# One core: float64 weights converted in even steps, unit results written in four pieces

## The chip, the cores and the metric

The kernel runs on one core of one Trainium2 chip. The metric is the device time of one execution in microseconds (us), the median of three runs. Below, PE is TensorE, DVE is VectorE, ACT is ScalarE, POOL is GpSimd and SP is the SyncE queue from which most transfers are issued. TensorE has two clock levels, 1.2 and 2.4 GHz; in the profile's rows the granted clock is 0.50 at the lower and 1.00 at the higher, and values between are means over a stretch.

## What is computed

Three stages follow one another, over 4 x 576 = 2304 tokens of width 512. The two weight matrices of the last stage, `w_in` and `w_out`, come as float64.

```python
def reference(**kw):
    attn = _attn_ref(q, k, v)            # 4 batches, 8 heads, 576 x 64, window of 64 keys
    x = attn.transpose(0, 2, 1, 3).reshape(2304, 512)
    x = _moe_ref(x, ...)                 # 8 experts, each token to the one of highest logit:
                                         #   gate * (relu(x @ w1[e]) @ w2[e]), 512 -> 1024 -> 512
    h = x @ w_in                         # 512 -> 2048, w_in float64
    return (h - tanh(h)) @ w_out         # 2048 -> 512, w_out float64
```

## The kernel before

**Attention** (`attention`) runs over 36 groups of four 128x128 score blocks. Beside it tokens are routed: `route_task` finds expert and gate, scaled rows go to `xs` in DRAM, and a table of units is made.

**The expert stage** (`moe`) works through 5 units, each up to 504 tokens of one expert (the last one 288), in 8 steps of 128 of the 1024 hidden columns: 40 steps, `p` = 0 to 39, `f` = `p` mod 8. A step multiplies twice: `l1` (PE into `ps_h`, 12 matmuls) and, for the step before, `l2` (into `ps_y`, 12 matmuls). The fp32 numbers are multiplied as high and low half: ACT rounds to the high half (`w1h`, `w2h`, `hh`, `xh`) and DVE subtracts to get the low half (`w1l`, `w2l`, `hl`, `xl`). Weights of step `p+3` and `p+2` are loaded by `wload` from SP into a ring of five buffers `r`, and a load waits until DVE has split the weights that lay there. At `f` = 7 the next unit's tokens are transposed on PE and split (`xsplit`, tiles `x`, `xh`, `xl`, four blocks in two buffers), and the results go to `ys` (`yevac`). At `f` = 2 of the next unit `ywrite` writes all of `ys` to `yd` in one DMA of 1008 KB, and the token ids, four bytes each, to `idd`. The next unit's tokens come by `xgather_task` (`xg`), four indirect DMAs issued from POOL.

**The conversion** (`conv_task`, a generator, one 512 KB block of float64 at a time, 16 of `w_in` and 16 of `w_out`) is a task among those that `Sched.pump` moves on. `conv_load` loads `raw` from SP (two buffers), one block ahead. `conv_low` turns the low word into a number on ACT (`cvr`); `conv_top` makes the fp32 of the high word in four DVE instructions (`cva`, L743 to L746, the first of them takes the absolute value); `conv_sum` adds the two on POOL (`cvw`, or `woutW` for the last 8 blocks, which stay whole). A block's high half (`winH`, `woutH`) is then made on ACT and its low half (`winL`, `woutL`) on DVE or POOL in turn. `cva`, `cvr` and `cvw` have one buffer each. The first ten blocks are converted during attention, the other 22 from `p` = 8 on, one in each step, at every `f`.

**The last stage** (`second`) goes over 6 chunks of 384 tokens and 16 blocks of hidden columns: `m2l1` (PE into `ps_g`, three buffers), `act1` (five ACT and five DVE instructions, the fourth of DVE, L1123, releases `ps_g`), `act2` (high half on ACT, low half on POOL), `m2l2` (into `ps_q`). In the first 8 steps the 8 blocks that stayed whole are split too, with the low half on POOL (L768). Its tiles take the place in SBUF of the expert stage's.

The order on each engine is the order in which the code issues; each engine's queue runs in order and waits for semaphores.

Of the kernel before, what the change touches and what calls it, by code (L numbers as in the profile page):

```python
# [23 lines left out]
NF1 = F // 128  # L24
# [20 lines left out]
CONV0 = 8  # L45
# [6 lines left out]
class Sched:  # L52


    def __init__(self):
        self.tasks, self.first = [], False

    def add(self, g, last=False):
        self.tasks.append([g, 0, last])
        if not self.first:  # L60
            self.tasks.sort(key=lambda t: t[2])
# [16 lines left out]
class Kernel:  # L78
    def __init__(self, tc, ap):
# [3 lines left out]
        self.woutH, self.woutW, self.conv_on = [], None, False  # L83
# [288 lines left out]
    def attention(self):  # L372
# [9 lines left out]
        for g in range(-2, NG + 2):  # L382
            n = g + 3
            self.useZ = g < NG
            if 0 < n < NG:
# [8 lines left out]
                if n == 6:  # L394
                    self.sched.add(self.conv_task(), last=True)
# [25 lines left out]
            self.sched.pump()  # L421

# [273 lines left out]
    def conv_task(self):  # L696
        tiles = [(0, f) for f in range(NF2)] + [(1, f) for f in range(NF2)]
        ready = lambda w, f: (f < NWA or self.conv_on) if w == 0 else f < len(self.woutH) or self.woutW
        raw, late = self.conv_load(*tiles[0]), None
        yield 3  # L700
        for i, (w, f) in enumerate(tiles):
            while not ready(w, f):
                yield
            nxt = tiles[i + 1] if i + 1 < len(tiles) else None
            cur, raw = raw, self.conv_load(*nxt) if nxt else None
            eng = self.nc.vector if i % 2 else self.nc.gpsimd
            r = self.conv_low(cur)
            if i < NWA:
# [3 lines left out]
                if late:  # L712
                    self.split_lo(hl, late[2], eng)
                a = self.conv_top(cur)
            else:
                a = self.conv_top(cur)
                if late:
                    self.split(*late, eng)
                yield
            late = self.conv_sum(w, f, a, r)  # L720
            yield
        if late:
            self.split(*late, self.nc.gpsimd)
        self.conv_done = True

# [12 lines left out]
    def conv_top(self, raw):  # L738
# [4 lines left out]
        v.tensor_scalar(a, hi, 0x7FFFFFFF, None, op0=ALU.bitwise_and)  # L743
# [23 lines left out]
    def split_lo(self, hl, w, eng):  # L767
        eng.tensor_tensor(hl[1], w, hl[0].bitcast(F32), op=ALU.subtract)  # L768

    def split(self, which, f, w, eng):  # L770
        self.split_lo(self.split_hi(which, f, w), w, eng)
# [27 lines left out]
    def xgather_task(self, u, Ti, k, rows=NT, spread=False):  # L799
# [3 lines left out]
        u.ids = mo.tile([BR, n], I32, name="ids", bufs=self.nbuf(4))  # L803
# [105 lines left out]
    def ywrite(self, u, yd, idd):  # L909
        self.nc.sync.dma_start(yd[:, :, bass.ds(u.c, u.C)], u.ys[:, :, : u.C])  # L910
        self.put_ids(idd, u.c, u)

    def moe(self):
# [8 lines left out]
        for p in range(N):  # L922
            self.conv_on = p >= CONV0
            if p == NF1 + 2:
                self.sched.tasks.sort(key=lambda t: not t[2])
                self.sched.first = True
# [26 lines left out]
            if i == 0:  # L953
                self.sched.pump()
# [335 lines left out]
```

## Time and profile before

| what | value |
|---|---|
| three timed runs | 850.59, 850.95, 854.36 us; median 850.95 us |
| the profiled execution | 853.73 us, of which 851.9 us span |
| PE busy | 780.5 us, 92% of the span |
| DVE, ACT, POOL busy | 77%, 61%, 34% of the span |

The span runs from the first to the last recorded instruction. Attention ends at about 165 us, the expert stage at about 430 us; the last stage fills the rest. "Busy" says nothing yet on what waits: that is read stage by stage, from the idle time of PE and what ended it.

### The profile page before, as it was taken

To read this page: it belongs to the slowest core of one execution; us is meant where nothing else is said; L and a number is where in the kernel's file an instruction comes from. 1 tells how busy PE (TensorE), PEld (TensorE's weight loads), DVE (VectorE), ACT (ScalarE), POOL (GpSimd) and SP (SyncE) were. 2 spreads that over 40 slices of the span, in tenths; PEclk is the share of its full clock that TensorE was granted. 3 is DMA by queue.
4 is the path that set the end of the run, shared out by engine and by line. 5 is a ranking of instruction groups with operands and counts; after the bars stand their busy time and mean duration, and the time that the engine had idled before them with its cause. 6 is when DMAs were issued, how large, how long until landed. Compare 5 with 4: busy or idle time off the path is not lost.

```text
span 851.9 us, 12816 instructions
## 1 busy us (share of the span) xinstructions
PE 780.5 (92%) x4183; PEld 677.4 (80%) x4183; DVE 656.4 (77%) x1144; ACT 522.3 (61%) x1246; POOL 285.8 (34%) x291
## 2 busy tenths in 40 slices
PE   7898989878997797899979999999999999999995
PEld 6877777657886686687969999999999999999993
DVE  4679986556397797767559888888888888888883
ACT  5878777623343443334467777777777777777772
POOL 3344443200252253231054424423423333333322
PEclk9999999989999898999999999999999999999998
DMA  6777975513376386393940101001001000000001
GB/s 143 182 185 193 234 160 138 168 62 125 121 232 162 116 229 192 122 228 113 194 64 1 37 1 38 29 10 38 28 10 38 20 20 31 17 11 13 25 2 41
DMA packets 119070, 80.35 MB, mean 94 GB/s; under 512 B 70688, under 2 KB 107040, under 8 KB 118994
## 3 DMA queue, kind: packets, MB, share of 16 engines
q1 hardware_dynamic: 115730, 69.81, 31.8%
q0 software_dynamic: 3264, 9.63, 3.4%
q8 instruction: 35, 0.57, 0.3%
q14 instruction: 41, 0.34, 0.1%
HBM read 62.10 MB, written 14.16 MB: 90 GB/s over the span
## 4 chain that ended last, share of the span: by engine, by line
PE 66%; DVE 14%; DMA 9%; ACT 4%; issue 3%; POOL 2%; SPq 1%; DVEq 0%; POOLq 0%; ACTq 0%
PE ps_g L1102 23%; PE ps_q L1145 23%; PE ps_h L864 7%; PE ps_y L881 6%; DMA raw<-in_wout 4%; ACT P L316 2%; PE ps_o L349 2%; DMA r<-in_w 1%; DVE nm L314 1%; PE ps_s L310 1%; DVE cva L744 1%; DVE w2l L855 1%; DVE w1l L855 1%; DMA idd<-ids 1%; DVE PT L334 1%
## 5 line engine op out<-in xcount | busy, mean ns | idle before, releaser
L1133 POOL TENSOR_TENSOR gl<-gv,gh 128x384 fp32r<-128x384 f32 x96 | 100.0, 1042 | 185.8 <-ACT gh L1132 185.6
L1102 PE MATMUL ps_g<-yh,winH 128*128 128x384 f32 x384 | 129.9, 338 | 6.0 <-DVE gt L1123 6.0
L1102 PE MATMUL ps_g<-yh,winL 128*128 128x384 f32 x384 | 129.9, 338 | 0.0
L1102 PE MATMUL ps_g<-yl,winH 128*128 128x384 f32 x384 | 129.9, 338 | 0.0
L1124 DVE COPY_PREDICATED gv<-gm,gt 128x384 f32<-128x384 int32 x96 | 112.1, 1167 | 9.9
L1145 PE MATMUL ps_q<-woutH,gl 128*128 128x512 f32 x288 | 114.1, 396 | 1.0 <-POOL gl L1133 1.0
L1145 PE MATMUL ps_q<-woutH,gh 128*128 128x512 f32 x288 | 114.2, 397 | 0.1
L1145 PE MATMUL ps_q<-woutL,gh 128*128 128x512 f32 x288 | 113.9, 395 | 0.0
L1132 ACT ACTIVATE gh<-gv 128x384 fp32r<-128x384 f32 x96 | 50.4, 525 | 102.7 <-issue 85.1
L1120 DVE SCALAR_TENSOR_TENSOR gv<-gu,ps_g 128x384 f32<-128x384 f32 x96 | 53.1, 553 | 43.4 <-ACT gt L1117 42.6
L1102 PEld LDWEIGHTS ps_g<-yh,winH 128*128 128x128 f32 x384 | 72.6, 189 | 10.5 <-DVE gt L1123 6.6
L1122 DVE SCALAR_TENSOR_TENSOR gv<-gs,gv 128x384 f32<-128x384 f32 x96 | 74.3, 774 | 3.3
L1102 PEld LDWEIGHTS ps_g<-yl,winH 128*128 128x128 f32 x384 | 72.7, 189 | 4.0
L1102 PEld LDWEIGHTS ps_g<-yh,winL 128*128 128x128 f32 x384 | 72.7, 189 | 0.0
L316 ACT ACTIVATE P<-ps_s,nm 128x128 f32<-128x128 f32 x144 | 50.9, 365 | 28.3 <-DVE nm L314 27.2
L753 ACT ACTIVATE cvr<-raw 128x512 int32<-128x512 uint32 x32 | 21.6, 675 | 72.2 <-POOL cvw L759 33.0
L1145 PEld LDWEIGHTS ps_q<-woutL,gh 128*128 128x128 f32 x288 | 54.5, 189 | 12.9
L1145 PEld LDWEIGHTS ps_q<-woutH,gl 128*128 128x128 f32 x288 | 54.3, 188 | 10.4 <-POOL gl L1133 1.7
L1145 PEld LDWEIGHTS ps_q<-woutH,gh 128*128 128x128 f32 x288 | 54.4, 189 | 9.3 <-ACT gh L1132 0.5
L1115 ACT ACTIVATE gs<-gu,pa 128x384 f32<-128x384 f32 x96 | 59.3, 617 | 3.1
L1121 DVE SCALAR_TENSOR_TENSOR gv<-gs,gv 128x384 f32<-128x384 f32 x96 | 58.1, 605 | 3.3
L1116 ACT ACTIVATE gs<-gu,pa 128x384 f32<-128x384 f32 x96 | 57.8, 602 | 1.6 <-DVE gv L1122 1.6
(254 smaller groups left out, 1737.5 us busy)
## 6 DMA issues: line engine op xcount, KB each, us to landing
r<-in_w SPq DMA_DIRECT2D x80, 256.0 KB, 3.8
raw<-in_win SPq DMA_DIRECT2D x16, 512.0 KB, 5.3
raw<-in_wout SPq DMA_DIRECT2D x16, 512.0 KB, 3.6
xs<-r SPq DMA_DIRECT2D x18, 256.0 KB, 2.6
kr<-in_k SPq DMA_DIRECT2D x32, 128.0 KB, 2.7
qr<-in_q SPq DMA_DIRECT2D x32, 128.0 KB, 3.8
va<-in_v SPq DMA_DIRECT2D x32, 128.0 KB, 3.1
yd<-ys SPq DMA_DIRECT2D x4, 1008.0 KB, 14.1
```

The source lines that it names most:

```text
L316: nc.scalar.activation(P[:, j, :], ps[:, j, :], AF.Exp, bias=nm[:, j : j + 1], accum_out=sm[:, j : j + 1])
L864: nc.tensor.matmul(ps, w[:, c, :], x[:, c, :n], start=(c == 0 and i == 0), stop=(c == 3 and i == 2))
L881: nc.tensor.matmul(u.y[d], w[:, d * 128 : d * 128 + 128], x, start=(f == 0 and i == 0), stop=(f == NF1 - 1 and i == 2),)
L1102: nc.tensor.matmul(ps, w[:, c, :], x[:, c, :], start=(c == 0 and i == 0), stop=(c == 3 and i == 2))
L1115: nc.scalar.activation(s1, u, AF.Square, bias=self.pa1)
L1116: nc.scalar.activation(s2, u, AF.Square, bias=self.pa2)
L1120: nc.vector.scalar_tensor_tensor(v, u, cA, ps, op0=ALU.mult, op1=ALU.mult)
L1121: nc.vector.scalar_tensor_tensor(v, s1, b1, v, op0=ALU.add, op1=ALU.mult)
L1122: nc.vector.scalar_tensor_tensor(v, s2, b2, v, op0=ALU.add, op1=ALU.mult)
L1124: nc.vector.copy_predicated(v, m.bitcast(I32), t)
L1133: nc.gpsimd.tensor_tensor(gl, v, gh.bitcast(F32), op=ALU.subtract)
L1145: nc.tensor.matmul(self.po[t], g[:, sl], w, start=(f == 0 and i == 0), stop=(f == NF2 - 1 and i == 2))
```

## The change

`conv_task` leaves the scheduler's list. `conv_step` moves it on by hand: once in each attention group, so that a block still takes two groups, and in the expert stage twice per step, one block, only at `f` = 1 to 6 and from `p` = 4 on. Blocks are loaded two ahead: at the end of block `i` block `i+2` is loaded, into the buffer that block `i` has just left. From the tenth block on the absolute value is made on ACT instead of DVE. All low halves are made on DVE, those at the start of the last stage too. `ywrite` writes one of the four column blocks of `ys` at each of `f` = 1, 2, 3 and 4, and the ids with the fourth. The ids' tile moves from the expert stage's pool to the constants.

```diff
-CONV0 = 8
+CONV0 = 4
+CONVF = (1, 2, 3, 4, 5, 6)
...
-                    self.sched.add(self.conv_task(), last=True)
+                    self.conv = self.conv_task()
...
             self.sched.pump()
+            self.conv_step()
...
-        raw, late = self.conv_load(*tiles[0]), None
+        raws, late = [self.conv_load(*t) for t in tiles[:2]], None
         yield 3
         for i, (w, f) in enumerate(tiles):
             while not ready(w, f):
                 yield
-            nxt = tiles[i + 1] if i + 1 < len(tiles) else None
-            cur, raw = raw, self.conv_load(*nxt) if nxt else None
-            eng = self.nc.vector if i % 2 else self.nc.gpsimd
+            cur = raws.pop(0)
             r = self.conv_low(cur)
             if i < NWA:
                 if late:
                     hl = self.split_hi(*late)
                 yield
                 if late:
-                    self.split_lo(hl, late[2], eng)
-                a = self.conv_top(cur)
+                    self.split_lo(hl, late[2])
+                a = self.conv_top(cur, False)
             else:
-                a = self.conv_top(cur)
+                a = self.conv_top(cur, True)
                 if late:
-                    self.split(*late, eng)
+                    self.split(*late)
                 yield
             late = self.conv_sum(w, f, a, r)
+            if i + 2 < len(tiles):
+                raws.append(self.conv_load(*tiles[i + 2]))
             yield
...
-        v.tensor_scalar(a, hi, 0x7FFFFFFF, None, op0=ALU.bitwise_and)
+        hf = raw.bitcast(F32).rearrange("p (n two) -> p n two", two=2)[:, :, 1]
+        if act:
+            self.nc.scalar.activation(x, hf, AF.Abs)
+        else:
+            v.tensor_scalar(a, hi, 0x7FFFFFFF, None, op0=ALU.bitwise_and)
...
-    def split_lo(self, hl, w, eng):
-        eng.tensor_tensor(hl[1], w, hl[0].bitcast(F32), op=ALU.subtract)
+    def split_lo(self, hl, w):
+        self.nc.vector.tensor_tensor(hl[1], w, hl[0].bitcast(F32), op=ALU.subtract)
...
-        u.ids = mo.tile([BR, n], I32, name="ids", bufs=self.nbuf(4))
+        u.ids = self.cp.tile([BR, n], I32, name="ids", bufs=4) if not self.few else mo.tile([BR, n], I32, name="ids")
...
-    def ywrite(self, u, yd, idd):
-        self.nc.sync.dma_start(yd[:, :, bass.ds(u.c, u.C)], u.ys[:, :, : u.C])
-        self.put_ids(idd, u.c, u)
+    def ywrite(self, u, yd, idd, d=None):
+
+        d = slice(0, 4) if d is None else slice(d, d + 1)
+        self.nc.sync.dma_start(yd[:, d, bass.ds(u.c, u.C)], u.ys[:, d, : u.C])
+        if d.stop == 4:
+            self.put_ids(idd, u.c, u)
...
-            self.conv_on = p >= CONV0
-            if p == NF1 + 2:
-                self.sched.tasks.sort(key=lambda t: not t[2])
-                self.sched.first = True
+            self.conv_on = True
...
             self.l1(u, f)
             self.sched.pump()
+            if f in CONVF and p >= CONV0:
+                self.conv_step()
...
                 self.l2(u, f - 1)
             self.sched.pump()
+            if f in CONVF and p >= CONV0:
+                self.conv_step()
...
-            if f == 2 and i > 0 or p == N - 1:
-                j = i - (f == 2)
+            if 1 <= f <= 4 and i > 0 or p == N - 1:
+                j = i - (p < N - 1)
...
-                self.ywrite(u, self.yd, self.idd)
+                self.ywrite(u, self.yd, self.idd, f - 1 if p < N - 1 else None)
...
-                    self.split(1, f + NF2 // 2, self.woutW[f].bitcast(F32), self.nc.gpsimd)
+                    self.split(1, f + NF2 // 2, self.woutW[f].bitcast(F32))
```

Three places show how it moves instructions. First SP, around the write of a unit's results (`yd`, `idd`), with the weight loads (`r`) and the block loads (`raw`) about it; before:

```order
L735 DMA raw<-in_wout 128x1024
L910 DMA yd<-ys 512x1x504
L903 DMA idd<-ids 126x4x1
L834 ISA
L834 DMA r<-in_w 128x4x128
L839 ISA
L839 DMA r<-in_w 128x512
L735 DMA raw<-in_wout 128x1024
```

Now, the fourth piece of the same write, with the ids:

```order
L742 DMA raw<-in_wout 128x1024
L923 DMA yd<-ys 128x504
L914 DMA idd<-ids 126x4x1
L805 TENSOR_LOAD tab
L845 ISA
L845 DMA r<-in_w 128x4x128
L850 ISA
L850 DMA r<-in_w 128x512
L742 DMA raw<-in_wout 128x1024
```

The other three quarters stand one step apart ahead of it, each behind a `raw` load; the `raw` load at the end is for the block of `f` = 1 of the next unit, where before it was for the next step.

Second DVE, at `f` = 7, where the next unit's tokens are split (`xl`); before:

```order
L870 SCALAR_TENSOR_TENSOR hl<-ps_h,hh 128x504
L743 TENSOR_SCALAR cva<-raw 128x512
L744 TENSOR_SCALAR cva<-cva 128x512
L745 TENSOR_SCALAR cva<-cva 128x512
L746 SCALAR_TENSOR_TENSOR cva<-raw,cva 128x512
L768 TENSOR_TENSOR woutL_2434<-cvw,woutH_2427 128x512
L825 TENSOR_TENSOR xl<-x,xh 128x504 x4
L896 COPY ys<-ps_y_3103 128x504
```

Now, from the last conversion of `f` = 6 on:

```order
L757 SCALAR_TENSOR_TENSOR cva<-raw,cva 128x512
L779 TENSOR_TENSOR woutL_2437<-cvw,woutH_2430 128x512
L866 TENSOR_TENSOR w1l<-r,w1h 128x512
L866 TENSOR_TENSOR w2l<-r,w2h 128x512
L881 SCALAR_TENSOR_TENSOR hl<-ps_h,hh 128x504
L836 TENSOR_TENSOR xl<-x,xh 128x504 x4
L907 COPY ys<-ps_y_3129 128x504
```

Between `hl` of `f` = 7 and `xl` there is no conversion any more; in the other steps L743 is gone and a low half (L779) stands in every step.

Third POOL, where the second unit's tokens are gathered (`xg`, four DMAs, at `f` = 5 and 6 of the first unit); before, from the last attention groups (`P`) on:

```order
L325 TENSOR_TENSOR P<-P,rc 128x512
L807 DMA xg<-xs,ids 126x512
L325 TENSOR_TENSOR P<-P,rc 128x512
L807 DMA xg<-xs,ids 126x512 x5
L768 TENSOR_TENSOR winL_87<-cvw,winH_77 128x512
L807 DMA xg<-xs,ids 126x512
L759 TENSOR_TENSOR cvw<-cva,cvr 128x512
```

Now, from the last attention group on:

```order
L324 TENSOR_TENSOR P<-P,rc 128x512
L770 TENSOR_TENSOR cvw<-cva,cvr 128x512
L818 DMA xg<-xs,ids 126x512 x2
L770 TENSOR_TENSOR cvw<-cva,cvr 128x512
L818 DMA xg<-xs,ids 126x512 x2
L770 TENSOR_TENSOR cvw<-cva,cvr 128x512
L818 DMA xg<-xs,ids 126x512 x4
L770 TENSOR_TENSOR cvw<-cva,cvr 128x512 x6
```

Of the five in a row before, four are the second unit's; now the sum of a block stands between its second and its third gather, and the third unit's four stand together.

## Rows read from the trace of the kernel before

**Rows 1.** The view by stretches, core 0; (x) is the instructions of each engine

```profile
core 0: us, PE busy (x) PEld busy (x) DVE busy (x) ACT busy (x) POOL busy (x), PEclk, DMA share, GB/s
...
225.00:445.00 220.00, 190.62 (x907) 160.72 (x905) 157.17 (x230) 96.05 (x181) 66.79 (x50) 0.94 0.62 162
```

**Rows 2.** The waits of TensorE, 225 to 470 us: total, times, longest

```profile
PE ps_h L864 <- ACT w1h L854: 13.6, 4, 5.1
PE x L822 <- DVE xl L825: 9.3, 2, 5.2
PE ps_g L1102 <- DVE gt L1123: 6.0, 2, 4.7
```

**Rows 3.** Windows, columns as in 1: six stalls, then undisturbed work

```profile
264.38:273.68 9.30, 4.35 (x14) 3.55 (x13) 5.99 (x8) 3.89 (x8) 2.56 (x2) 0.82 0.62 191
324.40:334.43 10.03, 4.92 (x13) 3.95 (x13) 6.53 (x9) 4.45 (x9) 2.87 (x2) 0.66 0.57 196
383.30:389.53 6.23, 4.40 (x13) 3.52 (x13) 5.50 (x9) 3.92 (x7) 1.59 (x1) 0.73 0.52 180
282.95:294.11 11.16, 5.95 (x20) 5.15 (x21) 7.25 (x12) 3.80 (x7) 2.11 (x2) 0.69 0.30 95
343.69:353.01 9.32, 5.24 (x20) 4.58 (x21) 6.14 (x11) 3.30 (x7) 1.58 (x2) 0.82 0.35 113
436.59:451.61 15.02, 9.03 (x34) 8.19 (x35) 11.32 (x16) 8.96 (x18) 6.64 (x6) 0.77 0.26 21
276.43:279.17 2.74, 2.74 (x13) 2.21 (x12) 2.74 (x4) 1.20 (x3) 1.50 (x1) 1.00 0.51 154
279.17:282.70 3.53, 3.53 (x21) 2.94 (x19) 3.43 (x6) 1.51 (x3) 1.79 (x2) 1.00 0.52 178
455.80:459.99 4.19, 4.19 (x22) 3.79 (x21) 3.88 (x6) 3.43 (x7) 2.59 (x3) 1.00 0.00 0
```

**Rows 4.** The chain that ended last, pieces between 255 and 450 us

```profile
263.34 7.16 DMA raw<-in_win
...
314.83 12.84 DMA raw<-in_wout
...
331.92 3.73 DMA raw<-in_wout
...
371.92 11.88 DMA raw<-in_wout
...
432.23 8.93 DMA idd<-ids
441.18 0.50 ACT gt L1117
```

**Rows 5.** Windows, columns as in 1: while the ids were written

```profile
316.00:323.00 7.00, 7.00 (x32) 5.78 (x31) 6.10 (x10) 2.32 (x5) 1.61 (x1) 1.00 1.15 125
```

**Rows 6.** The timeline of VectorE, 330 to 337 us

```profile
330.83 0.68 DVE L855 TENSOR_TENSOR w1l<-r,w1h 128x512 fp32r<-128x512 f32 x1
...
333.71 0.41 DVE L743 TENSOR_SCALAR cva<-raw 128x512 int32<-128x512 int32 x1
...
336.30 0.69 DVE L855 TENSOR_TENSOR w1l<-r,w1h 128x512 fp32r<-128x512 f32 x1
336.90 1.78 DVE L855 TENSOR_TENSOR w2l<-r,w2h 128x512 fp32r<-128x512 f32 x1
```

**Rows 7.** The timeline of GpSimd, 328 to 334 us

```profile
331.05 1.59 POOL L759 TENSOR_TENSOR cvw<-cva,cvr 128x512 int32<-128x512 int32 x1 [0.69 <-DVE cva L746]
```

**Rows 8.** The page, part 5, as its heading names the columns

```profile
L753 ACT ACTIVATE cvr<-raw 128x512 int32<-128x512 uint32 x32 | 21.6, 675 | 72.2 <-POOL cvw L759 33.0
```

**Rows 9.** The chain that ended last, a piece between 215 and 230 us

```profile
221.94 5.13 DMA xg<-xs,ids
```

**Rows 10.** The timeline of VectorE, 462 to 468 us

```profile
462.78 0.56 DVE L1120 SCALAR_TENSOR_TENSOR gv<-gu,ps_g 128x384 f32<-128x384 f32 x1
...
466.97 0.56 DVE L1120 SCALAR_TENSOR_TENSOR gv<-gu,ps_g 128x384 f32<-128x384 f32 x1 [0.46 <-ACT gt L1117]
```

More of the change, by code (lines that the diff above doesn't have):

```diff
@@ L55, in __init__, with add @@
     def __init__(self):
[L56 to L61, printed above, removed]
+        self.tasks = []
+    def add(self, g):
+        self.tasks.append([g, 0])
     def pump(self):
@@ L82, in __init__ @@
         self.raw, self.grp, self.nx, self.xrows, self.few = {}, {}, 0, 0, False
-        self.woutH, self.woutW, self.conv_on = [], None, False
+        self.woutH, self.woutW, self.conv_on, self.conv = [], None, False, None
     def pool(self, name, bufs, space=None, side=None):
@@ L712, in conv_task, with conv_step @@
                 if late:
-                    self.split_lo(hl, late[2], eng)
-                a = self.conv_top(cur)
+                    self.split_lo(hl, late[2])
+                a = self.conv_top(cur, False)
             else:
-                a = self.conv_top(cur)
+                a = self.conv_top(cur, True)
                 if late:
-                    self.split(*late, eng)
+                    self.split(*late)
                 yield
             late = self.conv_sum(w, f, a, r)
+            if i + 2 < len(tiles):
+                raws.append(self.conv_load(*tiles[i + 2]))
             yield
         if late:
-            self.split(*late, self.nc.gpsimd)
+            self.split(*late)
         self.conv_done = True
+    def conv_step(self):
+        if self.conv:
+            try:
+                next(self.conv)
+            except StopIteration:
+                self.conv = None
     def conv_load(self, which, f):
@@ L736, in conv_load, with conv_top @@
         return raw
-    def conv_top(self, raw):
+    def conv_top(self, raw, act):
         hi = raw.rearrange("p (n two) -> p n two", two=2)[:, :, 1]
@@ L765, in split_hi, with split @@
         return hi, lo
-    def split_lo(self, hl, w, eng):
-        eng.tensor_tensor(hl[1], w, hl[0].bitcast(F32), op=ALU.subtract)
-    def split(self, which, f, w, eng):
-        self.split_lo(self.split_hi(which, f, w), w, eng)
+    def split_lo(self, hl, w):
+        self.nc.vector.tensor_tensor(hl[1], w, hl[0].bitcast(F32), op=ALU.subtract)
+    def split(self, which, f, w):
+        self.split_lo(self.split_hi(which, f, w), w)
     def early_prep(self, j):
@@ L973, in moe @@
             if p == N - 4:
-                assert self.conv_done
+                while self.conv:
+                    self.conv_step()
+                    print("late conv")
                 self.es_cv.close()
```

## The prediction, made before the changed kernel ran

> **What bounds the kernel now.** I read the page's table of busy time first, then the slices, then the waits of TensorE by stretch. TensorE is busy for 92% of the span and no other engine for over 77%, so the time is TensorE's work plus what it waits. In the slices it stands still between 225 and 452 us only: there [rows 1] give 190.62 of 220 us busy at a mean granted clock of 0.94. In the last stage from 452 us on the idle time is near nothing at a granted clock of 1.00 (last row of [rows 3]). So nothing in the change shortens the last 400 us; what it can move is the expert stage and the seam behind it.
>
> There are two costs in each stop: the idle time, and the slow work behind it. A stretch around each of six stops [rows 3] shows both: 4.35 us busy in 9.30 at a mean clock of 0.82, 4.92 in 10.03 at 0.66, where the same instructions undisturbed take 2.74 us (12 matmuls into `ps_h`) at 1.00. 0.66 is a mean of both levels, 1.2 and 2.4 GHz: after the idle time TensorE works at the lower one for a while. So I price a stop as the length of its stretch minus what its instructions take undisturbed, and not by its idle time.
>
> Who ends the stops stands in the waits [rows 2]: four times ACT's `w1h` (13.6 us), twice DVE's `xl` (9.3), twice DVE's `gt` (6.0, the last stage's first steps). None of these engines is full; each holds the needed instruction behind another that waits. The chain that ended last names it.
>
> **What goes, term by term.**
>
> *A, the weights behind a late block.* ACT's `w1h` stands behind `cvr`, and `cvr` waits for `raw`. The chain holds `raw` landing after 7.16, 12.84 and 11.88 us, where it takes 3.73 undisturbed [rows 4]. Each of the three was issued behind `yd` in one 1008 KB piece and the 4-byte ids, at `f` = 2, for use in the next step. While the ids were written the DMA engines' share was 1.15 but only 125 GB/s moved [rows 5]: the engines are full of small pieces. The stops: 9.30 − 2.74 = 6.56, 10.03 − 2.74 = 7.29, 6.23 − 2.74 = 3.49 [rows 3], in sum 17.3 us. Now the `raw` load behind the ids is for a block used at `f` = 1 of the next unit, some four steps later, and the block for the step after the ids was loaded a step ahead of them. At 5.47 us a step (336.30 − 330.83 on DVE [rows 6]) four steps are 22 us of cover for a landing of at most 12.84. Gain **17.3**.
>
> *B, the change of unit.* At `f` = 7 TensorE transposes the next unit's tokens into two buffers and waits for `xl` on DVE, which stands behind `hl` and a whole conversion. 11.16 − 3.53 = 7.63 and 9.32 − 3.53 = 5.79 [rows 3], 13.4 us. There is no conversion at `f` = 7 or 0 now, so the five conversion instructions leave that place on DVE (front's second order). Gain **13.4**. There are four changes of unit; the first (`p` = 7) and the last (`p` = 31, after the last block) had no conversion ahead of `xl` before either, and [rows 2] count two such waits, not four.
>
> *C, the fourth `w1h` wait.* 13.6 us minus the idle time of the three of A (9.30 − 4.35 = 4.95, 10.03 − 4.92 = 5.11, 6.23 − 4.40 = 1.83 [rows 3]) is 1.7 us: weights behind the whole `yd` of the fourth unit. With a quarter a step: gain **1.7**, no clock loss counted.
>
> *D, the start of the last stage.* 436.59 to 451.61 is 15.02 us for one and a half steps (34 PE instructions, a step has 22 and takes 4.19): 15.02 − 1.5 × 4.19 = 8.7 lost [rows 3]. The chain there: the ids' DMA at 432.23 lands after 8.93, at 441.16, and ACT's `gt` starts at 441.18 [rows 4]: the last stage's tiles lie where the ids lay. In the constants the ids block nobody, so this wait goes. What comes next is DVE: a step's five instructions take 466.97 − 462.78 − 0.46 = 3.73 us [rows 10], and 8 steps get a low half more at 0.60 (336.90 − 336.30, the same subtraction [rows 6]): 4.33 us against PE's 4.19. That is 8 × 0.14 = 1.1 us late, and I leave one wait of about 2.1 (half the 4.7 of [rows 2], since the first step fills the pipeline anyhow). Gain 8.7 − 3.2 = **5.5**; ends 2 and 8.7.
>
> **What comes.**
>
> *E, the second unit's gathers.* POOL now does a block's sum between the second and third gather (third order in the section on the change): 1.59 us [rows 7], plus the wait for its operands. In the trace of before the last of these gathers was issued at 221.94 and landed after 5.13, at 227.07, and stands in the chain that ended last, so TensorE's transposes began when it came [rows 9]. So 1.6 to 2.2 us more are seen whole by TensorE, with slow work behind. The nearest row is the third stop of A, 1.83 idle and 3.49 in all. Loss **3.5**; ends 0 and 6 (as the second stop, 5.11 idle for 7.29).
>
> *F, engines that take over work.* Abs goes from DVE (0.41 us [rows 6]) to ACT for 22 blocks; a pass of 128x512 costs ACT 0.675 [rows 8]. In 225 to 445 us ACT is busy for 96 of 220 us [rows 1], so the 22 × 0.675 = 15 us are hidden there. DVE is the one to look at: in a step with its own low half the period is 5.47 [rows 6], as long as PE's. It loses 0.41 in every step and gains 0.60 where POOL did the low half; without the overlap with POOL it is relieved too, since `w2l` takes 1.78 beside POOL's sum and `w1l` 0.68 without [rows 6, 7], and POOL now does one instruction a block. So DVE's step is 5.47 − 0.41 = 5.06, under PE's. Nothing, ends −4 and +4. In attention four low halves go from POOL to DVE, 4 × 0.60 = 2.4 us, against about as much relief by the same overlap (1.78 − 0.69 = 1.1 each): nothing, within the same ends.
>
> *G, SP's queue.* `raw` for block `i+2` waits until DVE has read block `i`, and the weights of the next steps stand behind that wait. Weights are loaded two to three steps ahead, 11 to 16 us, and land in 3.7; a wait of one step still leaves 10.9 − 5.47 − 3.73 = 1.7. Nothing; this is the first rival.
>
> **Sum.** 17.3 + 13.4 + 1.7 + 5.5 − 3.5 = 34.4. The profiled execution took 853.73, so 819.3; it stands 2.78 above the median of 850.95, and I give the prediction against the median: 850.95 − 34.4 = **816.5 us**. The ends of D, E and F (2 to 8.7, 0 to 6, ±4) and A, which may not go whole, give 809 to 825 as the range of this case alone. The floor is 810: all of A to D without a cost is 41.1.
>
> **Rivals.**
>
> *1. The weights take the place of the blocks.* Behind the ids the queue now has weights first. If these land as late as `raw` did, ACT's `w1h` waits itself three times at `f` = 6 or 7: 3 × 7.29 = 21.9, or half of it. Against it: the same weights stood behind the ids before, and the waits name `raw`, not `r`, in the chain. Time 827 to 838. Chance 0.12. The Trainium skill, "DMA: Bandwidth & Descriptors", Specifications, says that pieces under 512 bytes cost a read-modify-write; the trace agrees as far as the ids' 4-byte pieces go with full engines at 125 GB/s [rows 5]. By that rule the ids stay as dear as they were.
>
> *2. The transitions stay.* `xl` may be late by `hl` and the four splits alone, as two buffers for four blocks make TensorE wait for DVE whatever stands ahead. B falls away: 830. Against it the two changes of unit without a conversion and without a wait. Chance 0.08.
>
> *3. Two ahead is not two ahead.* With two buffers the load of `i+2` starts when block `i` has been read, so the lead may be one step and the stops of A come back, less a quarter's shorter `yd`: 816.5 + 17.3 = 834. Against it the gap at `f` = 7 and 0, which gives two steps more. Chance 0.06.
>
> *4. Slower: the conversion becomes one chain.* Abs on ACT must follow POOL's last read of `cva`, and DVE's three must follow Abs, POOL's sum must follow them, and the high and low half follow that. `cva`, `cvr` and `cvw` have one buffer each, and ACT's and DVE's queues hold the weights' halves behind each link. Were a block's links to run in turn with nothing beside them, a step would need `cvr` and Abs 2 × 0.675, DVE's three about 1.4 (0.41, 0.41 and 0.60), the sum 1.59, the low half 0.60, and `w1l`, `w2l` and `hl` 0.60 + 1.78 + 0.60: about 7.9 us against 5.47, over 21 blocks 51 us: 850.95 − 34.4 + 51 = 868. It decides against the change from a period of 5.47 + 34.4 / 21 = 7.1 on. Against it: the links can run beside matmuls of the same step, a block is spread over two half steps, and before's odd steps hold all the same links but one in 5.47. Chance 0.05.
>
> *5. Quarters cost more than they free.* Each piece may hold the queue for its fixed time. If a transfer held it for a whole landing of 3.73 [rows 4], a step with two weight loads, a block and a quarter would need 4 × 3.73 = 15 us, over 5.47, and TensorE would wait in 12 steps: far slower, over 900. Against it: before already had three such transfers in 5.47 us. Chance 0.02. The Trainium skill, "DMA: Bandwidth & Descriptors", Bandwidth, advises batching to 1 MiB, with some 2 us fixed per transfer; by that 12 pieces more would be 24 us of queue, an estimate from the page, if nothing ran beside them. No row here shows a cost like it.
>
> **How the numbers follow.** The forecast holds 0.67: A to D go, E is paid. Rivals 1 to 3 are 0.26 together and lie at 827 to 838; 4 and 5 are 0.07. For 8 in 10 the range takes in the forecast's own 809 to 825 and most of 1 to 3: **809 to 835**. About 0.5% (4 us) is what a measurement of this kernel can tell from no change. Cases of 1 to 3 are all faster by more than that: faster 0.92, same 0.02, slower 0.06.
>
> **What would show it.** In the profile of the changed kernel: the waits of TensorE between 225 and 430 us should name neither `w1h` nor `xl` (A, B); if `w1h` is back with `r` as the chain's DMA it is rival 1, with `raw` rival 3. At the first change of unit TensorE's transposes should wait some 2 us for `xg` (E). At the start of the last stage no `idd` stands in the chain, and `ps_g` waits for `gt` at most some 2 us (D). The steps' pitch on TensorE in the expert stage should stay at about 5.5; 7 or more is rival 4. Were A's stops gone and the total unmoved, I'd look for a new stop in attention, where F was put at nothing.

## The result and the profile after

| | median of the runs | ratio to the kernel before, 95% interval | profiled execution |
|---|---|---|---|
| before | 851.10 us (850.59 to 854.36, 4 runs) | | 853.73 us |
| changed | 825.79 us (823.77 to 828.86, 4 runs) | 0.9698 [0.9659, 0.9737] | 823.77 us |

The change gains 25.3 us by the medians and 30.0 us between the two profiled executions; the one of before was 2.6 us over its median, the one of after 2.0 us under. Everything below that goes step by step compares profiled executions. The page of the changed kernel:

```profile
span 821.9 us, 12813 instructions
...
PE 770.2 (94%) x4183; PEld 670.7 (82%) x4183; DVE 644.8 (78%) x1142; ACT 535.8 (65%) x1268; POOL 261.0 (32%) x271
```

TensorE's busy time fell by 10.3 us (780.5 before), with the same 4183 instructions. Between the start of `p` = 7 and the last stage's sixth `ps_g` alone it fell from 198.8 to 187.8 us, and the mean granted clock there rose from 0.93 to 0.99: that is the work that no longer runs at the lower clock. The waits of TensorE from 215 to 470 us answer to [rows 2] (in total, times, longest):

```profile
PE ps_y L892 <- ACT hh L880: 4.7, 1, 4.7
PE ps_g L1119 <- DVE gt L1140: 2.0, 2, 1.7
PE x L833 <- DMA xg<-xs,ids: 1.6, 2, 1.1
```

`w1h` (13.6 us) and `xl` (9.3 us) are gone, `gt` fell from 6.0 to 2.0. New at the top is a wait for `hh`, ahead of the last `ps_y`. The windows that answer to [rows 1] and [rows 3] (us; busy and count of PE, PEld, DVE, ACT, POOL; granted clock, DMA share, GB/s) are the step of `p` = 13, a change of unit, the step ahead of the last stage, and an undisturbed step of the last stage:

```profile
261.35:266.82 5.47, 5.47 (x25) 4.52 (x24) 5.17 (x8) 3.42 (x7) 1.61 (x1) 1.00 0.80 232
272.31:282.28 9.97, 9.97 (x53) 8.41 (x52) 6.12 (x11) 4.38 (x9) 1.61 (x1) 1.00 0.83 244
394.61:405.68 11.07, 6.34 (x39) 6.10 (x37) 2.94 (x6) 4.03 (x9) 4.12 (x4) 0.85 0.53 58
...
429.15:433.36 4.21, 4.21 (x22) 3.79 (x21) 4.04 (x8) 3.55 (x9) 1.13 (x1) 1.00 0.00 0
```

The first two are full and at a clock of 1.00: no stop is left there. The third has 4.73 us without work. A ledger between the starts of the same matmuls on TensorE's timeline (the first `ps_h` of a step of the expert stage, the first matmul of a `ps_g` of the last stage) puts every microsecond in its place. Its last boundary is the sixth `ps_g`, since the first five come before or with the first work on `ps_q`:

| place | before | after | gain | forecast |
|---|---|---|---|---|
| from the start to `p` = 7 | 223.39 | 224.67 | −1.28 | F: 0 |
| first change of unit, `p` = 7 | 10.70 | 12.03 | −1.33 | E: −3.5 |
| `p` = 13 and 14, 21 and 22, 29 and 30 | 50.72 | 32.87 | 17.85 | A: 17.3 |
| changes of unit at `p` = 15 and 23 | 33.50 | 19.93 | 13.57 | B: 13.4 |
| `p` = 37 | 5.03 | 3.17 | 1.86 | C: 1.7 |
| `p` = 39 and the last stage up to its sixth `ps_g` | 26.22 | 26.15 | 0.07 | D: 5.5 |
| from there to TensorE's end | 391.10 | 392.16 | −1.06 | 0 |
| sum | | | 29.7 | 34.4 |

So three terms came within 0.6 us of their forecast, and 5.4 of the 34.4 us are lost in one row, D. That row has two parts that went opposite ways: `p` = 39, and the stretch from the first to the sixth `ps_g`, in which the stop lay that D priced. Before (same columns as above):

```profile
425.39:430.15 4.76, 4.76 (x38) 4.76 (x37) 2.57 (x4) 2.79 (x7) 4.06 (x4) 1.00 0.30 83
430.15:451.61 21.46, 15.46 (x72) 14.31 (x71) 14.03 (x20) 14.53 (x30) 10.18 (x9) 0.84 0.40 47
```

Now the second part is

```profile
405.68:420.76 15.08, 13.11 (x70) 12.05 (x70) 12.10 (x21) 12.91 (x27) 2.13 (x2) 1.00 0.62 68
```

It gained 6.4 us, more than the 5.5 of D, and `p` = 39 (the third window further up) lost 6.3: 11.07 us and not 4.76. The experiments go after that new stop first.

### The profile page after: what moved, and what is told of

It reads as the page before. It is cut to its first block, busy times and chain, and to the rows that moved or that the text cites. A ratio compares the mean times of both kernels' runs of the same rounds, so it can differ in the third digit from the quotient of the medians.

```text
span 821.9 us, 12813 instructions
## 1 busy us (share of the span) xinstructions
PE 770.2 (94%) x4183; PEld 670.7 (82%) x4183; DVE 644.8 (78%) x1142; ACT 535.8 (65%) x1268; POOL 261.0 (32%) x271
## 4 chain that ended last, share of the span: by engine, by line
PE 47%; issue 1%; DVE 1%; POOL 1%; ACT 0%; POOLq 0%; ACTq 0%; DVEq 0%
PE ps_g L1119 24%; PE ps_q L1162 24%; POOL out L1179 0%; POOL gl L1150 0%; DVE gv L1139 0%; DVE gv L1138 0%; DVE gt L1140 0%; DVE gv L1137 0%; ACT gs L1133 0%; ACT gt L1134 0%; DVE gv L1141 0%; DVE woutL L779 0%; POOLq L1022 0%; ACT woutH L775 0%; ACT gm L1136 0%
## 5 line engine op out<-in xcount | busy, mean ns | idle before, releaser
L1141 DVE COPY_PREDICATED gv<-gm,gt 128x384 f32<-128x384 int32 x96 | 108.9, 1135 | 10.2 <-DVE gt L1140 0.5
L770 POOL TENSOR_TENSOR cvw<-cva,cvr 128x512 int32<-128x512 int32 x24 | 34.3, 1430 | 125.7 <-DVE winL L779 67.5
L1132 ACT ACTIVATE gs<-gu,pa 128x384 f32<-128x384 f32 x96 | 59.3, 617 | 4.4 <-DVE gv L1138 1.2
L880 ACT ACTIVATE hh<-ps_h 128x504 fp32r<-128x504 f32 (+1 forms) x40 | 22.2, 554 | 58.9 <-PE ps_h L875 58.8
```

Of the source, the lines that this page charges most:

```text
L770: self.nc.gpsimd.tensor_tensor(w, a, r, op=ALU.add)
L880: nc.scalar.activation(hh, ps, AF.Relu)
L1132: nc.scalar.activation(s1, u, AF.Square, bias=self.pa1)
L1141: nc.vector.copy_predicated(v, m.bitcast(I32), t)
```

## The experiments

Where nothing else is said, the edit is to the changed kernel. The place "seam" is from the start of `p` = 37 to the last stage's sixth `ps_g`, so it holds C and D.

| run | median us | ratio to before, interval | start to `p` = 7 | change at `p` = 7 | `p` = 13 to 16 | `p` = 21 to 24 | seam |
|---|---|---|---|---|---|---|---|
| before | 851.1 | | 223.39 | 10.70 | 35.36 | 34.24 | 34.54 |
| before, again | 851.8 | | 222.76 | 10.56 | 34.60 | 34.07 | 34.91 |
| quarters alone | 841.4 | 0.986 [0.982, 0.990] | 221.00 | 10.26 | 31.86 | 30.06 | 35.94 |
| changed | 825.8 | 0.970 [0.966, 0.974] | 224.67 | 12.03 | 20.93 | 20.92 | 32.52 |
| changed, again | 825.5 | 0.969 [0.965, 0.973] | 226.54 | 11.58 | 20.93 | 20.93 | 31.39 |
| ids early | 825.4 | 0.969 [0.965, 0.973] | 222.95 | 22.31 | 20.91 | 21.35 | 26.19 |
| pause | 819.9 | 0.962 [0.958, 0.966] | 221.63 | 13.05 | 20.93 | 20.92 | 30.11 |
| both | 822.8 | 0.964 [0.961, 0.968] | 224.47 | 22.24 | 20.91 | 20.92 | 26.20 |
| three edits | 814.1 | 0.954 [0.947, 0.961] | 224.83 | 9.98 | 20.92 | 20.91 | 26.17 |
| whole yd | 828.8 | 0.972 [0.964, 0.979] | 225.68 | 14.92 | 22.25 | 24.19 | 30.28 |
| one ahead | 832.6 | 0.978 [0.971, 0.985] | 225.48 | 12.25 | 24.04 | 21.74 | 29.37 |
| every f | 832.0 | 0.976 [0.969, 0.983] | 225.03 | 10.84 | 28.16 | 26.29 | 29.20 |
| Abs on DVE | 822.2 | 0.962 [0.958, 0.966] | 227.17 | 14.87 | 20.92 | 20.93 | 32.67 |
| low halves on POOL | 828.2 | 0.971 [0.967, 0.974] | 223.90 | 13.72 | 20.92 | 21.54 | 31.03 |

The places are those of one profiled execution each, from the start of the first step named to that of the second; the medians are of one to six executions. The intervals of whole yd, one ahead, every f and low halves on POOL overlap that of the changed kernel: what these runs undo is told from the places in their traces and not from their medians.

### The same kernels once more

> The changed kernel a second time, for the spread of its stops. Theory (the ledger by steps of the first profile: A 17.9, B 13.6, C 1.9 gained, the seam to the last stage 0.1, the first change of unit -1.3, attention -1.3, last stage -1.1): the same stops at the same places, the stop ahead of the last ps_y of about 4.7 us idle and the one of ps_o at group 7 of about 3.8 us, 824 to 829 us. Rival (the 5 us between the two medians of prediction and result are chance of one execution): either stop is missing or half as long here.

The changed kernel took 825.53 us in the median. All its stops are where they were; their lengths moved: the wait for `hh` 3.1 and not 4.7 us, the seam 31.39 and not 32.52, the start up to `p` = 7 226.54 and not 224.67. The theory holds for the places, and a stop's length in one execution is good to about 2 us.

> The kernel before a second time. Theory (the profile that the prediction read was 2.8 us over the median because of the length of its stops, which the prediction subtracted at their length in that one execution): the six stops are 1 to 3 us shorter in sum, the time 849 to 852, and the last stage's steps are unchanged, about 4.19 us. Rival (the 2.8 us lie in attention or the last stage): the stops have the same lengths to 0.5 us.

The kernel before took 851.83 us. Against the execution that the prediction read, `p` = 13 to 16 and 21 to 24 were 0.9 us shorter in sum, the seam 0.4 longer, the stretch up to `p` = 7 0.6 shorter. The steps of the last stage were the same, 4.19 us. The three stops of A, the two of B and the seam were 0.9 us shorter in sum, just under the 1 to 3 us of the theory. Neither side is clean: of the 1.9 us between the two executions the shorter stops explain about half.

### Where term D went

The last step of the expert stage in the changed kernel, on ACT (start us, us; in brackets the idle time before and what ended it):

```profile
394.64 0.63 ACT L865 ACTIVATE w2h<-r 128x512 fp32r<-128x512 f32 x1 [3.37 <-DMA r<-in_w]
395.18 0.39 ACT L880 ACTIVATE hh<-ps_h 128x288 fp32r<-128x288 f32 x1
399.25 0.52 ACT L1099 ACTIVATE yh<-r 128x384 fp32r<-128x384 f32 x1 [3.68 <-DMA r<-yd]
401.27 0.52 ACT L1099 ACTIVATE yh<-r 128x384 fp32r<-128x384 f32 x1 [1.50 <-DMA r<-yd]
401.70 0.61 ACT L865 ACTIVATE w2h<-r 128x512 fp32r<-128x512 f32 x1
402.22 0.39 ACT L880 ACTIVATE hh<-ps_h 128x288 fp32r<-128x288 f32 x1
```

The last `w2h` and `hh`, for which TensorE waits until 402.66, stand behind `yh`: the split of the last stage's first rows, which waits for their load `r<-yd`. On SP, that load stands right behind the fourth quarter, the ids and one load of weights:

```profile
387.23 0.43 SPq L923 DMA_DIRECT2D yd<-ys  x1
387.70 0.46 SPq L914 DMA_DIRECT2D idd<-ids  x1
388.41 0.45 SPq L850 DMA_DIRECT2D r<-in_w  x1
389.82 1.00 SPq L1087 DMA_DIRECT2D r<-yd  x2
```

Its first two pieces were issued from 389.82 on, and the first `yh` began 9.4 us later; the third piece, issued at 392.02, took 9.85 us to landing. In between, the DMA engines were full and, from 392 on, moved little (the windows' last two columns):

```profile
390.00:392.00 2.00, 2.00 (x17) 2.00 (x17) 1.61 (x3) 1.04 (x2) 0.00 (x0) 1.00 1.36 204
392.00:394.00 2.00, 2.00 (x17) 2.00 (x17) 0.00 (x0) 0.00 (x0) 0.00 (x0) 1.00 0.87 52
394.00:396.00 2.00, 2.00 (x17) 2.00 (x16) 0.70 (x2) 0.93 (x2) 0.00 (x0) 1.00 0.94 55
396.00:398.00 2.00, 1.93 (x15) 1.69 (x13) 0.36 (x1) 0.00 (x0) 0.00 (x0) 1.00 0.96 66
```

What fills the engines is not the ids' own pieces. Counted packet by packet in this trace, the 4-byte packets take 9 ns each and 2% of the engines' time between 392 and 398 us. 91% goes to the 1536-byte packets of `r<-yd` itself: most take about 65 ns, but 55 of the 210 take over 0.5 us, up to 3.6.

Is it the ids or the quarter of `yd` that the load waits for? The second kernel moves the ids alone:

```diff
-        if d.stop == 4:
+        if d == slice(0, 4):
             self.put_ids(idd, u.c, u)
...
+            if f == 4 and i < len(order) - 1:
+                self.put_ids(self.idd, i * C, U[order[i]])
             if 1 <= f <= 4 and i > 0 or p == N - 1:
```

> The ids of a unit are written at f = 4 of that unit itself, one unit earlier than in the changed kernel (unit 3's at p = 28 and not at p = 36); the pieces of yd stay. Theory (TensorE's wait for hh before the last ps_y comes from the load of the first chunk's rows standing behind the 4-byte ids): r<-yd lands in 2 to 4 us and not 9.8, the wait of 4.7 us is gone, the step before the last stage takes 4.8 us and not 11.1, about 6 us less than the changed kernel, 819 to 821. Rival (the load waits for the last piece of yd itself, written at p = 36): nothing changes, 825.8. Second rival (another wait, for ps_g or the weights, takes its place): 823.

The wait for `hh` is gone, the seam fell from 32.52 to 26.19 us, by 6.3, and of the 1536-byte packets of `r<-yd` none takes over 0.62 us. So it was the ids; the quarter stayed where it was. The 6.3 us are the stop of one execution: over the seven profiled executions of a changed kernel whose ids stand there, `p` = 39 took 7.4 to 11.1 us, and 4.75 in this run. But the time stayed too (825.44): the ids of the first unit now went out at `p` = 4, ahead of the second unit's gathers, and cost more there than they gave back at the seam. The chain shows it, and TensorE's waits in the stretch from 215 us on:

```profile
222.91 12.83 DMA xg<-xs,ids
235.75 0.04 issue
235.79 1.31 PE x L833 x5
```

```profile
PE x L833 <- DMA xg<-xs,ids: 8.7, 4, 4.7
PE ps_g L1121 <- DVE gt L1142: 2.0, 2, 1.7
```

The gather took 12.83 us where it took 5.13 in the kernel before [rows 9], and the first change of unit 22.31 us and not 12.03. The expectation of 819 to 821 was wrong for that reason: the transfer's price was right, and that it is paid wherever something needed soon stands behind it was forgotten.

### The first block in attention

In the ledger's first row the changed kernel is late, though in attention only the low halves changed engines. Of all waits up to 176 us one is new on TensorE, and ACT has its cause (first TensorE's row, then ACT's):

```profile
39.03 0.49 PE L348 MATMUL ps_o<-PT,vb 128*128 128x128 f32 x2 [3.84 <-ACT xT L369]
```

```profile
36.13 0.68 ACT L764 ACTIVATE cvr<-raw 128x512 int32<-128x512 uint32 x1 [4.57 <-DMA raw<-in_win]
36.83 0.37 ACT L315 ACTIVATE P<-ps_s,nm 128x128 f32<-128x128 f32 x1
```

The generator says `yield 3` behind its first load. The scheduler's `pump` counted that 3; `conv_step` calls `next` and drops it. So the first conversion is issued in the next attention group: ACT stands ready for it at 31.56, and its load was issued at 31.23 and took 4.9 us. The third kernel puts the pause back:

```diff
-        yield 3
+        for _ in range(3):
+            yield
```

> The first block's conversion starts three attention groups after its load, as the generator's yield 3 meant; the changed kernel starts it one group after, since the hand-moved generator ignores the 3. Theory (the stop of 3.8 us on ps_o at group 7 is ACT's cvr waiting for the first raw): the stop is gone, group 7 comes 4.5 to 5 us earlier; of that 2 us are left at the end of attention and 1.3 us at the end of the first unit, so 1.3 to 2 us less than the changed kernel, 824. Rival (the routing work that is late for its own reasons sets the end of attention): no difference, 825.8.

The wait of 3.84 us for `xT` at that place is gone. `p` = 7 starts 3.0 us earlier than in the changed kernel, and the time fell to 819.85. That is more than the 1.3 to 2 us that were expected: in this pair of executions the start accounts for 3.0; the first change of unit gave 1.0 back; the seam was 2.4 us shorter, of which the repeat of the unedited kernel shows 1.1 without any edit. The intervals of the two kernels only touch, 0.958 to 0.966 against 0.966 to 0.974. How much of the wait reaches the expert stage is not shown: `p` = 7 starts at 222.95 to 227.17 in the eight executions without the pause and at 221.63, 224.47 and 224.83 in the three with it.

> Both edits, the ids of a unit written one unit earlier and the pause of three groups. Theory: the two are at different places and add up, 6 + 1.3 to 2 us less than the changed kernel, 818. Rival for the first: only the pause's share, 824; for the second: only the ids' share, 820.

The two edits do not add up: 822.78 us. The seam is 26.20 as expected and the change of unit 22.24: the cost of the ids ahead of the gathers again.

A kernel with three edits, then: the pause stays, the ids of unit 3 alone go out early, at `p` = 30, and with the conversion of `p` = 5 POOL's sum leaves the place between the gathers. Its new lines:

```diff
-            if f in CONVF and p >= CONV0:
+            if f in CONVF and p >= CONV0 and p != 5:
...
+            if f == 6 and i == len(order) - 2:
+                self.put_ids(self.idd, i * C, U[order[i]])
...
-                self.ywrite(u, self.yd, self.idd, f - 1 if p < N - 1 else None)
+                self.ywrite(u, self.yd, self.idd, f - 1 if p < N - 1 else None, i < len(order) - 1 or p == N - 1)
...
-        if d.stop == 4:
+        if ids and d.stop == 4:
```

> The changed kernel with three edits: the pause of three groups ahead of the first block; no conversion at p = 5, so that POOL's sum doesn't stand between the second unit's gathers; the ids of unit 3 alone written one unit earlier (p = 30, not p = 36), those of the other units where the changed kernel has them. Theory: the seam's step is back at 4.75 us (as with all ids early), the first change of unit at 10.7 us (as in the kernel before) and not 22 as with unit 0's ids ahead of the gathers; from the pause alone (819.9) the seam gives 4 and the change of unit 2.3 us, 813 to 815. Rival (the gathers are late by their own 5 us and not by POOL's order): 816. Rival (ids at p = 30 hold up the last unit's weights): 820 or more.

814.10 us, inside the expected 813 to 815 and 11.7 us under the changed kernel: ratio to the kernel before 0.954 [0.947, 0.961], a version that beats both. The seam is 26.17, the first change of unit 9.98, with no wait for the gathers. All that TensorE waits for between 215 and 470 us is now:

```profile
PE ps_g L1122 <- DVE gt L1143: 2.0, 2, 1.7
PE ps_y L893 <- DVE w2l L867: 0.3, 1, 0.3
```

With POOL's sum out of the way the four gathers follow one another as before, and the sum comes behind:

```profile
219.03 1.04 POOL L819 DMA_INDIRECT xg<-xs,ids  x1 [2.02 <-DVE w1l L867]
220.38 1.40 POOL L819 DMA_INDIRECT xg<-xs,ids  x1 [0.31 <-issue]
222.08 1.00 POOL L819 DMA_INDIRECT xg<-xs,ids  x1 [0.30 <-issue]
223.38 0.99 POOL L819 DMA_INDIRECT xg<-xs,ids  x1 [0.30 <-issue]
226.55 1.59 POOL L771 TENSOR_TENSOR cvw<-cva,cvr 128x512 int32<-128x512 int32 x1 [2.17 <-DVE winL L780]
```

In this execution attention was 3.1 us longer at its end than in the run with the pause alone, by small waits and slower stretches with no one cause that the profile names: the pause ends the wait at its place, and its worth for the whole stage stays open.

### Which part of the change took A away

Three kernels undo one part each, one makes one part alone. First the whole `yd` and ids at `f` = 2 again:

```diff
-            if 1 <= f <= 4 and i > 0 or p == N - 1:
+            if f == 2 and i > 0 or p == N - 1:
...
-                self.ywrite(u, self.yd, self.idd, f - 1 if p < N - 1 else None)
+                self.ywrite(u, self.yd, self.idd)
```

> The changed kernel with one part undone: yd and the ids are written whole at f = 2 again. Theory (two steps of lead and not the quarters end the stops of A): w1h waits no more than 2 us each behind a block, the fourth w1h wait of about 1.9 us is back, and the seam's stop is shorter since unit 3's ids go out two steps earlier: 821 to 829. Rival (the quarters end A): three stops of 3.5 to 7.3 us are back, 838 to 843.

828.82 us, in the expected range. At `f` = 5 to 6 TensorE has no stop; but the weights now land late (ACT's `w1h` waits 4.14 us, over the 2 of the theory, then it catches up), and the delay comes out at the change of unit, 11.30 and 13.23 us and not 9.97. `p` = 37, term C, is 5.63 us again, and the ids at `f` = 2 leave the seam without its stop before the last `ps_y`.

```profile
269.12 0.63 ACT L865 ACTIVATE w1h<-r 128x512 fp32r<-128x512 f32 x1 [4.14 <-DMA r<-in_w]
...
271.26 0.67 ACT L764 ACTIVATE cvr<-raw 128x512 int32<-128x512 uint32 x1 [0.51 <-DMA raw<-in_wout]
```

Second, one block of lead and not two:

```diff
-        raws, late = [self.conv_load(*t) for t in tiles[:2]], None
+        raws, late = [self.conv_load(*tiles[0])], None
...
+            if i + 1 < len(tiles):
+                raws.append(self.conv_load(*tiles[i + 1]))
             cur = raws.pop(0)
...
-            if i + 2 < len(tiles):
-                raws.append(self.conv_load(*tiles[i + 2]))
```

> The changed kernel with one part undone: a block is loaded one step ahead, as before; quarters and places of the conversions stay. Theory (the lead ends A): the block of f = 6 stands behind the ids of f = 4 with one step of lead, three stops of 3.5 to 7.3 us on w1h or hh, 838 to 846. Rival (the quarters end A, or the ids alone are cheap): within 2 us of the changed kernel, 824 to 828.

832.58 us, between the theory's 838 and the rival's 828. ACT waits for the block of `f` = 6:

```profile
275.54 0.66 ACT L764 ACTIVATE cvr<-raw 128x512 int32<-128x512 uint32 x1 [4.17 <-DMA raw<-in_wout]
```

The step itself is 5.49 us on TensorE all the same; what is late comes out behind it, at the change of unit: 13.08 and 10.79 us. The profiled execution was the fastest of the five, 7.3 us under their median; where the others lost more is not shown.

Third, the quarters alone, on the kernel before:

```diff
-        self.nc.sync.dma_start(yd[:, :, bass.ds(u.c, u.C)], u.ys[:, :, : u.C])
-        self.put_ids(idd, u.c, u)
+        self.nc.sync.dma_start(yd[:, d, bass.ds(u.c, u.C)], u.ys[:, d, : u.C])
+        if d.stop == 4:
+            self.put_ids(idd, u.c, u)
...
-            if f == 2 and i > 0 or p == N - 1:
+            if 1 <= f <= 4 and i > 0 or p == N - 1:
```

> The kernel before with one part of the change alone: yd in four pieces at f = 1 to 4, the ids with the fourth; blocks one ahead and at every f. Theory (lead and quarters share A, since a block with one step of lead still stands behind the ids but no longer behind 1008 KB): the three stops of A are there, 3 to 5 us each and not 3.5 to 7.3, B is whole (13.4 us), the fourth w1h wait is gone: 838 to 847. Rival (the ids alone make A): no gain, 849 to 852. Rival (yd's 1008 KB alone make A): 17 to 19 us gained, 832 to 834.

841.39 us, 9.7 us under the table's kernel before and 11.9 under the median of 853.26 that was taken beside it: where the theory had it, but not in the way it said. The three stops of 3.5 to 7.3 us are not shortened, they are gone at their place (11.20 us for `p` = 13 and 14, 10.96 undisturbed), and the change of unit is longer, 20.66 us and not 17.68: ACT waits 5.91 us for the block of `f` = 6, and behind it is the conversion of `f` = 7, and behind that `xl`.

```profile
273.07 0.68 ACT L753 ACTIVATE cvr<-raw 128x512 int32<-128x512 uint32 x1 [5.91 <-DMA raw<-in_wout]
```

So the lead or the quarters, either of them, end the stops at `f` = 5 and 6, and neither takes away all of the delay: with the lead and the whole `yd`, 1.3 and 3.3 us stay at the changes of unit, and C; with the quarters and one block of lead 3.1 and 0.8 us in the profile, 7 in the median. The prediction gave A to the lead; the runs don't allow that. C goes with the quarters in every run. With the quarters the ids also go out two steps later, and no run here moves one without the other.

Fourth, a conversion in every step:

```diff
-CONV0 = 4
-CONVF = (1, 2, 3, 4, 5, 6)
+CONV0 = 8
+CONVF = (0, 1, 2, 3, 4, 5, 6, 7)
```

> The changed kernel with one part undone: one block in each step from p = 8 on, at f = 7 and 0 too; loads two ahead, quarters, Abs and low halves stay. Theory (the conversion ahead of xl makes B): the changes of unit at p = 15 and p = 23 take 15.8 to 17.7 us again and not 9.97, TensorE waits for xl on DVE, 13 us more, 839. Rival (B went because Abs and the freed queue make DVE faster): 826 to 830.

The changes of unit are 17.21 and 15.34 us, 12.6 more than in the changed kernel, and TensorE waits for `xl` again: term B is what the conversions at `f` = 7 and 0 cost, as the theory has it.

```profile
PE x L833 <- DVE xl L836: 8.0, 2, 4.6
```

The time of 832.01 and not 839 is explained in part: with `CONV0` = 8 no sum stands between the gathers and the first change of unit is 10.84 us, and the seam is 3.3 us shorter, whose length differs from run to run.

### Abs and the low halves

```diff
-                a = self.conv_top(cur, True)
+                a = self.conv_top(cur, False)
```

> The changed kernel with one part undone: the absolute value on DVE for all blocks. Theory (DVE has 0.4 us to spare in a step, the changes of unit have no conversion): steps of 5.48 us on TensorE, within 2 us of the changed kernel, 824 to 828. Rival (DVE becomes the bound, 0.41 us late in each of 21 steps): 834.

```diff
+            eng = self.nc.vector if i % 2 else self.nc.gpsimd
...
-                    self.split_lo(hl, late[2])
+                    self.split_lo(hl, late[2], eng)
...
-                    self.split(*late)
+                    self.split(*late, eng)
```

> The changed kernel with one part undone: a block's low half on GpSimd and DVE in turn, as before, in attention and the expert stage (the last stage's first eight stay on DVE). Theory (neither engine bounds a step): 824 to 828, steps of 5.48 us; the second unit's gathers up to 1 us later where a low half stands between them too. Rival (DVE is held up beside GpSimd, as w2l of 1.78 us beside its sum): two more instructions of DVE stretched in every second step, 829 or more.

The medians are 822.16 and 828.19 us with spreads of 10 and 5 us, the one under the expected 824 to 828, the other at its upper end; the steps at `p` = 13 to 16 are 20.92 in both, so neither rival is seen there. Neither part moves a step of the expert stage, but with low halves on POOL one change of unit, `p` = 23, takes 10.59 us and not 9.97. With Abs on DVE, the engine's step is as long as TensorE's (300.01 to 305.49 is 5.48) and has no idle time; on ACT, it is 5.34 us there with 0.22 of waiting. The first two rows are with Abs on DVE, the next two the changed kernel:

```profile
300.01 0.67 DVE L881 SCALAR_TENSOR_TENSOR hl<-ps_h,hh 128x504 fp32r<-128x504 f32 x1
...
305.49 0.67 DVE L881 SCALAR_TENSOR_TENSOR hl<-ps_h,hh 128x504 fp32r<-128x504 f32 x1
```

```profile
300.08 0.67 DVE L881 SCALAR_TENSOR_TENSOR hl<-ps_h,hh 128x504 fp32r<-128x504 f32 x1
300.98 0.43 DVE L755 TENSOR_SCALAR cva<-cva 128x512 f32<-128x512 f32 x1 [0.22 <-ACT cva L752]
...
305.42 0.67 DVE L881 SCALAR_TENSOR_TENSOR hl<-ps_h,hh 128x504 fp32r<-128x504 f32 x1
```

Whether Abs on ACT costs something elsewhere stays open: the median without it is 3.6 us lower, but the interval touches that of the changed kernel.

## Why the prediction was right, and where it was not

The forecast of 816.5 us missed the 825.8 by 9.3; the range of 809 to 835 held it. Half of the 9.3 is terms, 4.7 us; the other half, 4.6, is that a sum made from one execution each lies 2.6 us from the one median and 2.0 from the other. That the range held it is in part luck: the terms' own ends, 809 to 825, miss the 825.8 narrowly, and the upper end of 835 was there for rivals 1 to 3, none of which occurred.

**A, B and C** were right in size: 17.85, 13.57 and 1.86 us against 17.3, 13.4 and 1.7. Pricing a stop by its stretch minus the undisturbed work held: the idle times of [rows 3] alone would have given 11.9 us for A. B is shown by the run with a conversion in every step. The cause given for A, the lead of four steps, was too narrow (the quarters with the later ids remove the same stops), and the delay can come out at the change of unit. Two readings there were wrong too. Of the three late blocks the first (7.16 us) is not the one that ACT waited for ahead of the first stop: that one was issued at 255.29, and ACT began on it 12.3 us later. And it was not so that the engines were "full of small pieces" [rows 5]: in that window the 4-byte packets make up 3% of the engines' time; the rest is ordinary packets, of which dozens take 0.5 to 2.6 us.

**D** was right for the stretch it priced (6.4 us of gain against 5.5): the idle time for `gt` fell from 6.0 to 2.0 us, as the 2.1 left for one wait had it, and quarters alone, which leaves the ids' tile in its old pool, keeps 5.6. The step that failed is "in the constants the ids block nobody". Their tile blocks nobody there, but their transfer does: the change moved it from `f` = 2 to `f` = 4 of the last unit, close ahead of the load of the last stage's first rows, and a step there is 3.2 us. That made a new stop of 6.3 us at `p` = 39. The working followed the queue behind the ids for blocks and for weights (rival 1), and did not ask what else is issued behind them in the last unit. The price was there: the ids took 8.93 us [rows 4]. The Trainium skill, "DMA: Bandwidth & Descriptors", Specifications, puts 512 bytes as the least piece for full rate. The trace agrees as to the rate, 4 bytes in 9 ns where 512 bytes take 27 ns, but the time was lost in the larger packets behind.

**E** has the right place and cause. In all seven executions with the sum between the gathers, and no ids ahead of them, the last gather is issued within 0.12 us of the start of `p` = 7, and 1.45 us ahead of it in the five without that sum; the change of unit takes 11.6 to 14.9 us in the seven and 10.0 to 10.8 in the five. So the loss is 0.9 to 4.2 us over the 10.70 of before: the ledger's 1.33 lies near its low end, and the 3.5 of the forecast within.

**F** was nothing in the expert stage, as forecast, and not in attention. The step that failed counted instructions, their engines and their cost, and not when the generator is moved: the dropped `yield 3` made a new wait of 3.84 us, of which an unknown part reaches the expert stage.

**G** and the rivals: no weight is late at `f` = 6 or 7, the unit changes are clean, and steps are 5.48 us; rivals 1 to 5 did not occur. With the whole `yd` the late weights of rival 1 do occur (4.14 us), and with one block of lead the late block of rival 3 does.

The Trainium skill, "GPSIMD Engine Reference", Specifications, says that GpSimd shares SBUF interfaces with VectorE, with contention for DVE instructions with two SBUF inputs. The trace agrees: `w2l` takes 1.78 us beside POOL's sum, 0.69 without. Both kernels have that one in a step; before, every second step had another, `cva` (L746) with 1.76 us beside POOL's low half, which went with it. TensorE's step is 5.48 us either way.

## What to carry to other kernels

Moving a transfer moves its queue: for each load issued behind it at its new place, in every stage and in the shortest steps, ask what waits for it. A delay that several edits shorten has no single owner, and it shows at the next place without slack, so undo the parts one at a time before giving each its share. When a task leaves a scheduler, look for what the scheduler did with its yields.

## What was not expected of the hardware

The ids are 2 KB in pieces of four bytes, written from SP, and they delayed not only loads behind them on SP (up to 9.85 us to landing, 2.3 to 4.0 where the ids stand elsewhere) but gathers issued from POOL: the last one landed after 12.83 us, and after 5.13 in the kernel before. In both places the 4-byte packets themselves took 9 ns each, and right behind them packets of other transfers that mostly take 27 to 84 ns took up to 3.6 us (at the seam) and 5.7 us (ahead of the gathers). Why is not shown.

From the eighteenth `ps_g` of the last stage to its last, TensorE took 326.39 us in all three kernels whose ids lie in the expert stage's pool (before, before again, quarters alone) and 327.23 us in all eleven whose ids lie among the constants (the two groups differ in more than that), at a granted clock of 1.00 and without a wait; that is 0.84 of the 1.06 us in the ledger's last row. The same matmuls run there. The lengths of the steps recur: in the changed kernel the first four blocks take 4.20 us in the second, fourth and sixth chunk and 4.14 in the third and fifth, and the chunks take turns in two sets of tiles for their rows. So it could be where tiles lie in SBUF; it was not tried.
